# Sparse attention and a squared-ReLU layer on one core: the last four squares of the first half batch taken in place in slot 8, its last transpose on TensorE, one key load and eight output pieces moved

## The chip, the cores and the metric

The kernel runs on one core of a Trainium2 chip. The core has five engines that run side by side, each through its own list of instructions in order: TensorE (PE, matrix products; its weight loads have a row of their own, PEld), VectorE (DVE), ScalarE (ACT), GpSimd (POOL) and SyncE (SP, which here only issues transfers). They hand work to each other by semaphores. Products land in PSUM banks, which the other engines empty; everything else lies in SBUF, filled from and written to HBM by DMA.

The metric is the device time of one execution in microseconds (us). Before the change the median of three runs is 269.56 us (269.19 to 270.07).

## What is computed

Queries, keys and values have 4 batches, 8 heads, 768 tokens and 64 columns. For each query the 24 chunks of 32 keys get an upper bound of their score from each chunk's smallest and largest key; the six best chunks are kept, and attention runs over these alone, causally. The result, 3072 tokens of 512 columns, goes through a layer with a squared ReLU.

```python
ub = sum(max(q * k_min, q * k_max))        # per query and chunk, causal
top_chunks = argsort(ub)[..., -6:]
scores = where(chunk of key in top_chunks and key <= query, q @ k.T / 8, -1e9)
x = softmax(scores) @ v                     # reordered to 3072 x 512
h = maximum(x @ w_in, 0)                    # 512 -> 2048
out = (h * h) @ w_out                       # 2048 -> 512
```

## The kernel before

**Slots.** Work is cut into 32 slots, numbered from 0. A slot is one pair of heads for 384 queries, which is half of a batch. Four slots make a half batch, `hb = s // 4`; `ORDER` puts them as batch 0 first half (slots 0 to 3), batch 1 first half (4 to 7), batch 0 second half (8 to 11), batch 1 second half (12 to 15), and so on. "The ninth slot" is slot 8, and "the tenth pair" belongs to slot 9. A manual schedule is used: each engine runs its instructions in the order in which the program text issues them. The loop over slots (from 4 on) is that order, written by hand.

**Attention of a slot.** For slot `s` the loop runs, among others:

- `step_E(s, hh, n)` (L452, L458, L462): scores of head `hh`, bank `n`, on PE into a PSUM tile `ps`; ACT takes the exponent into `e`; for `n == 1` POOL zeroes the part above the diagonal (the affine select).
- `step_U(s+1)` (L375, L382, then DVE L389, L391): the bounds `ub` of the next slot on PE, the maxima and the choice of chunks on DVE.
- `step_V(s+1)` (L434, L439): the choice turned by PE into `qt`, copied by DVE into the queries' extra rows of `kq`.
- `step_F(s-1)` (L478, then DVE L487, L488): the product with the values, `po`, for the slot before, and its division into `x`.
- `step_P(s+2)` (L267): keys and queries of the slot after next turned by PE into `tk` and `tq`; then `relus_T` (ACT, L288), `extrema` (DVE, L228 to L233: smallest and largest keys) and `place` (L293: keys by DVE, queries by ACT). For slot 9 these last steps stand at the head of slot 8 instead, around `step_F(7)`.

From half batch 3 on (`ON_PE`), keys and queries are not turned by PE but by transposes of DMA that SP issues (`tr`, L320, into `kqT`). For half batch 3 the loads are `load_n` (L109, issued by POOL): three of keys (`j` = 0, 1, 2) in slot 7, three of queries in slot 8. SP issues the three transposes of keys at the start of slot 9, the three of queries at the start of slot 10, and `place_dma` (L306) at the start of slot 11. On SP's list the transpose of `x` of slot 8 stands between the keys' and the queries' transposes. The readers are DVE: `step_K` (L336, smallest and largest keys of half batch 3, from slot 10 on) and `relus` (L316, L317, `qr` of slot 12), which `step_U(12)` in slot 11 needs.

**The layer.** `x` of a half batch is turned into `xT`: pair by pair by a transpose of DMA that SP issues right after `step_F` (L492), except for half batch 0, where PE does it (`x_T`, L516, into a PSUM tile `pt` that DVE copies, `x_copy`, L522). `push(hb)` then puts the layer's pieces of that half batch in a queue: 16 "up" pieces (`ffn_up`, L563: four matmuls of 384 columns into `ph`, ReLU by ACT into `ht`, L567, the square by DVE into `h`, L569) and 12 "down" pieces (`ffn_down`, L581: four matmuls of 512 columns into `py`, three tiles `t` of four steps `c`; step `c` needs the squares 4c to 4c+3; the last step is followed by a copy to `ob`, L587, and the write to `out`, L591). The downs of a half batch are queued among the ups of the next one; the first four of them follow its own ups at once (`LAG`). `f1()` takes one piece off the queue, if the slot's `quota` allows; so these pieces fill PE between the steps of the attention.

PSUM is tight: `psF` has two banks (`ph`, in the first slots also `tk`, `pt`, and the second output tile of half batch 0), `psY` one (`py`, and for slots 5 to 8 the transposed keys or queries), `psS` three (`ps`), `psA` two (`ub`, `qt`, `po`, later `tq`). In slot 7, piece (0, 0) of the downs takes the bank of `psY` that holds `tk` of slot 8 until DVE has copied it (L293).

**Numbers that the change touches.** `quota` by pair: half batch 1 (5, 5, 4, 4), half batch 2 (8, 6, 7, 5). Through slot 7 the queue has given up pieces 0 to 15 of half batch 0 and the downs (0, 0), (0, 1); (1, 0) and (1, 1) follow in slot 8.

Of the kernel before, what the change touches and what calls it, by code (L numbers as in the profile page):

```python
# [9 lines left out]
BF16 = mybir.dt.bfloat16  # L10
AX = mybir.AxisListType
ALU = mybir.AluOpType
ACT = mybir.ActivationFunctionType
# [4 lines left out]
HB = HT * 128  # L18
# [21 lines left out]
def kernel(  # L40
# [9 lines left out]
    nc = tc.nc  # L50
# [3 lines left out]
    NP = H // 2  # L54
# [3 lines left out]
    NFI = DFF // 128  # L58
# [153 lines left out]
    def col_of(half, j, i):  # L212
        for n, bank in enumerate(BANKS[half]):
            for (at, jj, i0, m) in bank:
                if jj == j and i0 <= i < i0 + m:
                    return 512 * n + at + 128 * (i - i0)
        raise KeyError

    slots = [(b, half, p) for b, half in ORDER for p in range(NP)]
    NS = len(slots)  # L220
# [16 lines left out]
    def in_order(x):  # L237

        return x.rearrange("r (j p) -> r p j", j=TP)

    def by_token(x):
        return x.rearrange("r (p j) -> r p j", j=TP)
# [47 lines left out]
    def place(s, n, copy, h0=0, h1=2):  # L290
        b, half, p = slots[s]
        for h in range(h0, h1):
            copy(by_token(kqs[b % 2][0:D, p, 2 * half + "kq".index(n), h, :]),  # L293
                 in_order(st[s][n][D * h:D * h + D]))
# [54 lines left out]
    F, Y, A = (psF, "ph"), (psY, "py"), (psA, "att")  # L349
# [92 lines left out]
    def step_E(s, hh, n):  # L442
# [17 lines left out]
        if n == 1:  # L460
# [2 lines left out]
                out=d, in_=d, compare_op=ALU.is_ge, fill=0.0, base=0,  # L463
                channel_multiplier=-1, pattern=[[0, 3], [1, 128]])

    xs = {}

    def step_F(s, hh):
        b, half, p = slots[s]
        t = st[s]  # L470
        if hh == 0:
            t["po"] = psA.tile([128, 2, HT, D + 1], F32, tag="att", name="po")
        po = t["po"]
        for i in range(HT):
            iq = HT * half + i
            for j in range(iq + 1):
                c = col_of(half, j, iq)
                nc.tensor.matmul(  # L478
                    po[:, hh, i, :], lhsT=t["e"][hh][:, c:c + 128],
                    rhs=vn[b % 2][:, 2 * p + hh, j, :],  # L480
                    start=(j == 0), stop=(j == iq))
        if hh == 1:
            if p == 0:
                xs[s // NP] = work.tile([128, NP, HT, 128], BF16, tag="x", name="x")
            x = xs[s // NP]
            r = work.tile([128, 2, HT, 1], F32, tag="r", name="r")
            nc.vector.reciprocal(r, po[:, :, :, D:D + 1])  # L487
            nc.vector.tensor_mul(  # L488
                x[:, p].rearrange("p j (h d) -> p h j d", h=2),
                po[:, :, :, 0:D], r.to_broadcast([128, 2, HT, D]))  # L490
            if s // NP and s < NS - 1:
                nc.sync.dma_start_transpose(  # L492
                    out=xT_of(s // NP)[:, p, :].rearrange("r (j t) -> r j t", j=HT),
                    in_=x[:, p].rearrange("p j t -> p (j t)"))
            st.pop(s)
# [3 lines left out]
    h2 = {}  # L499
# [3 lines left out]
    def xT_of(hb):  # L503
        if hb not in xTs:
            xTs[hb] = late.tile([128, NKI, HB], BF16, tag="xT", name="xT")
        return xTs[hb]
# [3 lines left out]
    def x_T(hb, g, pt, us=(0, 1)):  # L510

        if (hb, g) not in pts:
            pts[hb, g] = pt[0].tile([128, 2, HB], BF16, tag=pt[1], name="pt")
        for u in us:
            for j in range(HT):
                nc.tensor.matmul(  # L516
                    pts[hb, g][:, u, 128 * j:128 * (j + 1)],
                    lhsT=xs[hb][:, 2 * g + u, j, :],
                    rhs=ident, is_transpose=True, start=True, stop=True)

    def x_copy(hb, g, u0, u1, copy):
        copy(xT_of(hb)[:, 2 * g + u0:2 * g + u1, :], pts[hb, g][:, u0:u1, :])  # L522

    def push(hb):
        xT = xTs.pop(hb)
        xs.pop(hb)
        ups = [lambda act, f=f: ffn_up(hb, xT, f) for f in range(NFI)]
        for c in ("u" * NFI if hb == 0 else
                  "dddd" + "uuud" * 4 + "uuuu" if hb < 2 * B - 1 else
                  "uudddd" + "uuud" * 4 + "uu"):  # L530
            queue.append((ups if c == "u" else downs).pop(0))
        downs.extend(ffn_downs(hb, int(hb == 2 * B - 1)))
        if hb < 2 * B - 1:
            queue.extend(downs.pop(0) for _ in range(LAG))

    def ffn_downs(hb, tail=False):
        py = {}
        order = [(t, c) for t in range(HT - tail) for c in range(4)]
        if hb == 0:

            order = [(0, 0), (0, 1), (1, 0), (1, 1), (0, 2), (0, 3), (1, 2), (1, 3)] + order[8:]
        return [lambda act, t=t, c=c: ffn_down(hb, py, t, c, act, tail) for t, c in order]

    def ffn_last(hb):
# [15 lines left out]
    def ffn_up(hb, xT, f):  # L560
        ph = psF.tile([128, 512], F32, tag="ph", name="ph")
        for ki in range(NKI):
            nc.tensor.matmul(  # L563
                ph[:, 0:HB], lhsT=w_in[:, ki, 128 * f:128 * (f + 1)],
                rhs=xT[:, ki, :], start=(ki == 0), stop=(ki == NKI - 1))
        ht = late.tile([128, HB], BF16, tag="ht", bufs=4, name="ht")
        nc.scalar.activation(ht, ph[:, 0:HB], ACT.Relu)  # L567
        h = late.tile([128, HB], BF16, tag="h", bufs=2 * NFI + 2, name="h")
        nc.vector.tensor_mul(h, ht, ht)  # L569
        h2[hb, f] = h  # L570

# [29 lines left out]
    def at(s, fn, *a):  # L601
        later.setdefault(s, []).append(lambda: fn(*a))
# [21 lines left out]
        at(3 + g, load_w_out, 8 * g, 8 * g + 8)  # L624
    for j in range(HT):
        at(6, load_vt, 0, HT + j)
        at(7, load_n, "k", 3, j)
        at(8, load_n, "q", 3, j)
        at(9, load_vt, 1, HT + j)
    at(9, codes, 1, 1, nc.gpsimd.dma_start)  # L630
# [59 lines left out]
    late = ctx.enter_context(tc.tile_pool(name="late", bufs=2))  # L690
# [44 lines left out]
    for s, (b, half, p) in enumerate(slots):  # L735
        if s < NP:
            continue
        hb = s // NP
        nb = len(BANKS[half])
        hf = nb // 2  # L740
        quota = [((5, 5, 4, 4) if hb == 1 else (8, 6, 7, 5) if hb == 2 else (8, 6, 7, 7))[p]]
        for fn, *a in first.get(s, ()):
            fn(*a)
        if (hb == ON_PE - 1 and p == 2) or (ON_PE < hb < 2 * B - 1 and p == 0):
# [2 lines left out]
        def f1():  # L747
            if quota[0] and queue:
                quota[0] -= 1
                fill(1, True)  # L750
# [12 lines left out]
        if s == 2 * NP:  # L763
            for n in range(hf):
                step_E(s, 0, n)
            relus_T(s + 1)
            place(s + 1, "q", nc.scalar.copy)
            step_F(s - 1, 0)
            step_F(s - 1, 1)
            push(1)  # L770
            f1()
            f1()
            extrema(s + 1)
            place(s + 1, "k", nc.vector.tensor_copy)
        if p == 0 and hb > 2:
            step_F(s - 1, 0)
            step_F(s - 1, 1)
            push(hb - 1)
        else:
            f1()  # L780
# [26 lines left out]
                .rearrange("p i h j c -> p (i h j) c"), 0.0)  # L807
        late_f = half == 0 and hb > 2
        border = p == 0 and hb > 1
        if not border and not (late_f and p == NP - 1):  # L810
            f1()
        if p and s > NP:
            step_F(s - 1, 0)
# [88 lines left out]
```

## Time and profile before

The profiled execution took 269.26 us; its span, from the first to the last instruction, is 267.5 us. The median of the runs shown is 0.30 us above that execution.

| | busy us | share of the span | instructions |
|---|---|---|---|
| PE (matmul) | 254.6 | 95% | 2406 |
| PEld (weight load) | 156.3 | 58% | 2406 |
| DVE | 163.4 | 61% | 617 |
| ACT | 177.5 | 66% | 398 |
| POOL | 93.6 | 35% | 140 |

How it is read: a row of the timeline gives start, length, engine, line, operation, names and shapes, and how many instructions were merged; in square brackets stand the idle time of the engine just before and what is taken to have ended it. Matmuls overlap, so a row's length reaches into the next row. The granted clock of PE was full in all of the 40 slices. A row "in windows" gives, for a stretch of time, the busy time of each engine in it.

### The profile page before, as it was taken

How to read it: one execution, taken by the hardware profiler on the slowest of the kernel's cores; microseconds unless marked ns; L12 is line 12 of the kernel's file. 1: busy time of each engine (PE TensorE's matmuls, PEld its weight loads, DVE VectorE, ACT ScalarE, POOL GpSimd, SP SyncE). 2: the span in 40 equal slices, each digit the busy share in tenths (PEclk: the TensorE clock that was granted, in tenths of full speed). 3: DMA queues.
4: the chain of work that ended last, by engine and by line, in shares of the span. 5: the costliest groups of instructions: out<-in, count | busy, mean ns of one | idle time of the engine just before them, and what ended most of it. 6: DMA issues, size and time to landing. Idle time of an engine off the chain costs nothing.

```text
span 267.5 us, 6575 instructions
## 1 busy us (share of the span) xinstructions
PE 254.6 (95%) x2406; PEld 156.3 (58%) x2406; DVE 163.4 (61%) x617; ACT 177.5 (66%) x398; POOL 93.6 (35%) x140
## 2 busy tenths in 40 slices
PE   7878998889999999999999999999999999999995
PEld 6565554446656566665565566655565566645543
DVE  6789998565997458656875567455863233424411
ACT  4888986597895578845575787944685788614500
POOL 8897455524931325325521444220120111000000
PEclk9999999999999999999999999999999999999999
DMA  7999999999997599999996899998542220111022
GB/s 141 159 175 182 207 214 193 113 165 117 133 131 158 124 151 185 121 195 141 187 153 137 130 145 176 109 164 144 134 101 69 71 44 18 54 43 39 0 81 78
DMA packets 116849, 33.98 MB, mean 127 GB/s; under 512 B 103760, under 2 KB 112752, under 8 KB 116816
## 3 DMA queue, kind: packets, MB, share of 16 engines
q0 software_dynamic: 64672, 13.83, 72.4%
q1 hardware_dynamic: 51200, 19.33, 41.0%
q10 hardware_dynamic: 944, 0.39, 0.6%
q8 instruction: 19, 0.31, 0.5%
q14 instruction: 14, 0.11, 0.2%
HBM read 27.26 MB, written 6.29 MB: 125 GB/s over the span
## 4 chain that ended last, share of the span: by engine, by line
PE 75%; DVE 7%; DMA 6%; issue 4%; ACT 4%; POOL 3%; POOLq 0%; DVEq 0%; ACTq 0%
PE py L581 26%; PE ph L563 24%; PE ps L452 10%; PE po L478 7%; DMA xT<-x 3%; DMA kn<-in_k_dram 3%; PE idle L657 2%; ACT e L458 2%; POOL kn L109 1%; PE ub L375 1%; PE py L551 1%; ACT ht L567 1%; POOL e L462 1%; DVE km L336 1%; DVE x L488 1%
## 5 line engine op out<-in xcount | busy, mean ns | idle before, releaser
L458 ACT ACTIVATE e<-ps 128x512 bf16<-128x512 f32 x192 | 96.4, 552 | 19.3 <-PE ps L452 18.4
L563 PE MATMUL ph<-xT,w_in 128*128 128x384 bf16 x512 | 98.7, 325 | 1.7 <-DMA xT<-x 1.2
L581 PE MATMUL py<-w_out,h 128*128 128x512 bf16 x368 | 88.1, 379 | 0.9 <-DVE kq L293 0.7
L567 ACT ACTIVATE ht<-ph 128x384 bf16<-128x384 f32 x128 | 62.4, 500 | 28.6 <-PE ph L563 27.8
L569 DVE TENSOR_TENSOR h<-ht 128x384 bf16<-128x384 bf16 x128 | 46.6, 375 | 55.8 <-ACT ht L567 55.2
L462 POOL TENSOR_SCALAR_AFFINE_SELECT e<-e 128x384 bf16<-128x384 bf16 x64 | 34.1, 538 | 125.8 <-ACT e L458 122.2
L563 PEld LDWEIGHTS <-w_in 128*128 128x128 bf16 x512 | 47.7, 97 | 32.7 <-issue 2.7
L452 PE MATMUL ps<-kq 96*128 96x384 bf16 (+2 forms) x320 | 57.4, 278 | 2.1 <-DVE kq L428 2.1
L581 PEld LDWEIGHTS <-h 128*128 128x128 bf16 x368 | 34.6, 97 | 35.9 <-DVE kq L293 0.8
L452 PEld LDWEIGHTS <-kq 96*128 96x128 bf16 x320 | 26.3, 97 | 16.9 <-issue 2.2
L478 PEld LDWEIGHTS <-e 128*128 128x128 bf16 x672 | 25.4, 98 | 6.2 <-POOL e L462 1.6
L478 PE MATMUL po<-vn,e 128*128 128x65 bf16 x672 | 27.0, 194 | 1.6 <-POOL e L462 1.0
L587 ACT COPY ob<-py 128x512 f32<-128x512 f32 x18 | 10.5, 585 | 25.4 <-PE py L581 25.1
L389 DVE MAX8 m<-ub 128x8 f32<-128x16 f32 (+4 forms) x160 | 16.1, 166 | 17.0 <-PE ub L382 11.1
L488 DVE TENSOR_TENSOR x<-po,r 128x384 bf16<-128x384 f32 x32 | 17.8, 557 | 1.1
L109 POOL DMA_DIRECT2D kn<-in_k_dram x15 | 13.4, 901 | 3.0 <-ACT e L458 2.6
L109 POOL DMA_DIRECT2D qn<-in_q_dram x15 | 13.2, 889 | 0.3
L125 POOL DMA_DIRECT2D vn<-in_v_dram x15 | 12.5, 840 | 2.2 <-ACT qr L288 2.0
L336 DVE TENSOR_TENSOR km<-km 128x384 bf16<-128x384 bf16 (+3 forms) x40 | 12.2, 304 | 1.1
L375 PE MATMUL ub<-kbd,qr 128*128 128x48 bf16 (+1 forms) x160 | 9.9, 180 | 1.5 <-DVE kbd L233 0.9
L375 PEld LDWEIGHTS <-qr 128*128 128x128 bf16 x160 | 7.8, 96 | 5.6 <-DVE qr L316 1.5
L288 ACT ACTIVATE qr<-tq 128x256 bf16<-128x256 bf16 (+1 forms) x24 | 8.8, 422 | 0.9 <-PE tq L260 0.7
(71 smaller groups left out, 178.0 us busy)
## 6 DMA issues: line engine op xcount, KB each, us to landing
out_dram<-ob SPq DMA_DIRECT2D x23, 256.0 KB, 2.5
w_in<-in_moe_w_in_dram POOLq DMA_DIRECT2D x2, 1024.0 KB, 12.2
w_out<-in_moe_w_out_dram POOLq DMA_DIRECT2D x2, 1024.0 KB, 19.3
kn<-in_k_dram POOLq DMA_DIRECT2D x15, 128.0 KB, 6.7
qn<-in_q_dram POOLq DMA_DIRECT2D x15, 128.0 KB, 6.7
kq<-kqT SPq DMA_DIRECT2D x10, 192.0 KB, 5.3
vn<-in_v_dram POOLq DMA_DIRECT2D x4, 384.0 KB, 8.4
vn<-in_v_dram POOLq DMA_DIRECT2D x9, 128.0 KB, 9.7
```

What stands on the lines that cost most here:

```text
L109: nc.gpsimd.dma_start(out=nat_of(n, g)[:, DM * j:DM * j + DM].rearrange("p (h d) -> p h d", d=D), in_=rows(n, *ORDER[g], 0, H)[:, 128 * j: ...
L375: nc.tensor.matmul(ub[:, j - j0], lhsT=st[s]["qr"][:, w, 128 * j:128 * (j + 1)], rhs=kbds[b % 2][:, p, w, :, 0:ncs], start=bool(half) and ...
L389: nc.vector.max(out=m8[:, j, hh, :], in_=ub[:, j - j0, hh, 0:12 * half + 4 * j + 4])
L452: nc.tensor.matmul(ps[:, at:at + 128 * m], lhsT=kqs[b % 2][0:KR, p, 2 * (j // HT), hh, 128 * (j % HT):128 * (j % HT + 1)], rhs=qc(s, hh)[: ...
L458: nc.scalar.activation(e[:, 512 * n + lo:512 * n + hi], ps[:, lo:hi], ACT.Exp, scale=float(scale))
L462: nc.gpsimd.affine_select(out=d, in_=d, compare_op=ALU.is_ge, fill=0.0, base=0, channel_multiplier=-1, pattern=[[0, 3], [1, 128]])
L478: nc.tensor.matmul(po[:, hh, i, :], lhsT=t["e"][hh][:, c:c + 128], rhs=vn[b % 2][:, 2 * p + hh, j, :], start=(j == 0), stop=(j == iq))
L488: nc.vector.tensor_mul(x[:, p].rearrange("p j (h d) -> p h j d", h=2), po[:, :, :, 0:D], r.to_broadcast([128, 2, HT, D]))
L563: nc.tensor.matmul(ph[:, 0:HB], lhsT=w_in[:, ki, 128 * f:128 * (f + 1)], rhs=xT[:, ki, :], start=(ki == 0), stop=(ki == NKI - 1))
L567: nc.scalar.activation(ht, ph[:, 0:HB], ACT.Relu)
L569: nc.vector.tensor_mul(h, ht, ht)
L581: nc.tensor.matmul(py[t], lhsT=h2[hb, f][:, 128 * t:128 * (t + 1)], rhs=w_out[:, f, :], start=(f == 0), stop=(f == NFI - 1))
```

## The change

- **Squares.** The last four up pieces of half batch 0 (`f` = 12 to 15) no longer square at once. ACT writes the ReLU straight into `h`, the square is kept in a list `squares`, and DVE takes the four in place in slot 8, behind `extrema` and `place` of slot 9's keys. Before, two of them stood in slot 6 and two in slot 7 on DVE.
- **Last transpose of half batch 1.** For slot 7, SP no longer transposes `x`; PE does it (`x_T`, three matmuls into a bank of `psF`), and DVE copies it into `xT` behind the four squares. `push(1)` stands behind that copy.
- **Order of pieces.** In slot 7 no piece is taken ahead of `step_F(6)`. The downs of half batch 0 run (0,2), (1,2), (0,3), (1,3) instead of (0,2), (0,3), (1,2), (1,3). The queue of half batch 1 begins with six downs instead of four, then five ups, a down, five ups, a down and six ups. The quota of half batch 2 is (8, 5, 6, 7) instead of (8, 6, 7, 5).
- **One key load.** The third load of keys for half batch 3 moves from slot 7 to slot 8, and there, on POOL's list, it follows the select of `step_E(8, 1, 1)`, between the second and the third load of queries. POOL's order there becomes: two key loads, three selects, two query loads, a select, the key load, the third query load.

Everything that is computed stays; SP issues one transpose less, PE three matmuls more, DVE one copy more.

```diff
@@ step_F
-            if s // NP and s < NS - 1:
+            if s // NP and s < NS - 1 and s != 2 * NP - 1:
                 nc.sync.dma_start_transpose(
@@ push
         for c in ("u" * NFI if hb == 0 else
+                  "dddddd" + "u" * 5 + "d" + "u" * 5 + "d" + "u" * 6 if hb == 1 else
                   "dddd" + "uuud" * 4 + "uuuu" if hb < 2 * B - 1 else
@@ ffn_downs
-            order = [(0, 0), (0, 1), (1, 0), (1, 1), (0, 2), (0, 3), (1, 2), (1, 3)] + order[8:]
+            order = [(0, 0), (0, 1), (1, 0), (1, 1), (0, 2), (1, 2), (0, 3), (1, 3)] + order[8:]
@@ ffn_up
+        h = late.tile([128, HB], BF16, tag="h", bufs=2 * NFI + 2, name="h")
+        if hb == 0 and f >= NFI - 4:
+            h2[hb, f] = h
+            nc.scalar.activation(h, ph[:, 0:HB], ACT.Relu)
+            squares.append(lambda: nc.vector.tensor_mul(h, h, h))
+            return
         ht = late.tile([128, HB], BF16, tag="ht", bufs=4, name="ht")
         nc.scalar.activation(ht, ph[:, 0:HB], ACT.Relu)
-        h = late.tile([128, HB], BF16, tag="h", bufs=2 * NFI + 2, name="h")
         nc.vector.tensor_mul(h, ht, ht)
@@ loads
-        at(7, load_n, "k", 3, j)
+        at(7 + j // 2, load_n, "k", 3, j)
@@ loop over slots
-        quota = [((5, 5, 4, 4) if hb == 1 else (8, 6, 7, 5) if hb == 2 else (8, 6, 7, 7))[p]]
+        quota = [((5, 5, 4, 4) if hb == 1 else (8, 5, 6, 7) if hb == 2 else (8, 6, 7, 7))[p]]
@@ s == 2 * NP
             step_F(s - 1, 0)
             step_F(s - 1, 1)
-            push(1)
-            f1()
+            f1()
+            x_T(1, 1, F, (1,))
             f1()
             extrema(s + 1)
             place(s + 1, "k", nc.vector.tensor_copy)
+            for fn in squares:
+                fn()
+            x_copy(1, 1, 1, 2, nc.vector.tensor_copy)
+            push(1)
@@ ahead of step_F
-        if not border and not (late_f and p == NP - 1):
+        if not border and not (late_f and p == NP - 1) and s + 1 != 2 * NP:
             f1()
```

1 line of the change is left out of this document (added).

## The prediction, made before the changed kernel had run

> **What bounds the kernel now.** I read the shares of the engines first, then the windows, to see where PE stands still, then PE's timeline there. PE is the busiest engine, and after 85.14 us it is idle for 174.86 - 174.47 = 0.39 us in all: nothing is to be had there. Between 42.00 and 60.49 us it is idle for 18.49 - 15.11 = 3.38 us, in the next stretch for 0.47.
>
> ```profile
> PE 254.6 (95%) x2406; PEld 156.3 (58%) x2406; DVE 163.4 (61%) x617; ACT 177.5 (66%) x398; POOL 93.6 (35%) x140
> 42.00:60.49 18.49, 15.11 (x142) 8.26 (x140) 12.41 (x42) 12.39 (x28) 8.26 (x12) 1.00 2.62 154
> 60.49:85.14 24.65, 24.18 (x287) 15.93 (x285) 20.55 (x84) 19.74 (x44) 12.21 (x17) 1.00 1.62 139
> 85.14:260.00 174.86, 174.47 (x1484) 103.75 (x1482) 93.58 (x359) 110.44 (x239) 42.98 (x62) 1.00 0.92 112
> ```
>
> PE's timeline names four waits in the first stretch, and they are all of it: 0.47 + 0.72 + 0.99 + 1.20 = 3.38. In order: the bounds of slot 8 wait for DVE, the first down piece for DVE's copy of keys (which frees its bank), the second head of `step_F(7)` for POOL's select, an up piece of half batch 1 for the transpose of `x`.
>
> ```profile
> 43.10 0.31 PE L375 MATMUL ub<-kbd,qr 128*128 128x48 bf16 x6 [0.47 <-DVE kbd L233]
> ...
> 44.14 1.04 PE L581 MATMUL py<-w_out,h 128*128 128x512 bf16 x4 [0.72 <-DVE kq L293]
> 45.01 0.54 PE L478 MATMUL po<-vn,e 128*128 128x65 bf16 x12
> 45.39 1.03 PE L581 MATMUL py<-w_out,h 128*128 128x512 bf16 x4
> ...
> 49.34 0.36 PE L478 MATMUL po<-vn,e 128*128 128x65 bf16 x6 [0.99 <-POOL e L462]
> 49.54 3.61 PE L581 MATMUL py<-w_out,h 128*128 128x512 bf16 x16
> 52.99 0.55 PE L452 MATMUL ps<-kq 96*128 96x128 bf16 x3
> ...
> 58.94 1.71 PE L563 MATMUL ph<-xT,w_in 128*128 128x384 bf16 x9 [1.20 <-DMA xT<-x]
> ```
>
> So a change here is worth what it takes off these four, less what it makes PE wait elsewhere.
>
> **Squares out of slots 6 and 7.** On DVE two of them stand ahead of slot 8's keys:
>
> ```profile
> 39.75 0.35 DVE L569 TENSOR_TENSOR h<-ht 128x384 bf16<-128x384 bf16 x1
> ...
> 40.71 0.35 DVE L569 TENSOR_TENSOR h<-ht 128x384 bf16<-128x384 bf16 x1
> ...
> 42.97 1.11 DVE L293 COPY kq<-tk 64x384 bf16<-64x384 bf16 x2
> 44.00 0.61 DVE L569 TENSOR_TENSOR h<-ht 128x384 bf16<-128x384 bf16 x2
> ```
>
> DVE has no idle time there, so without a pair (0.61 merged) everything behind it is 0.61 earlier: the bounds no longer wait 0.47, and the copy of keys ends at 44.08 - 0.61 = 43.47. PE is free for the down piece 0.47 earlier too, at 44.14 - 0.72 - 0.47 = 42.95, and the change puts `step_F(6)` there (45.39 - 45.01 = 0.38), which fills the wait: down piece at 43.5, end at 43.5 + 0.87 = 44.4, where before piece and product ended at 45.39. Gain 1.0.
>
> **The third key load out of slot 7.** It holds POOL until 48.74, when the select starts for which PE waits 0.99:
>
> ```profile
> 47.85 0.89 POOL L109 DMA_DIRECT2D kn<-in_k_dram  x1 [2.62 <-ACT e L458]
> 48.74 1.04 POOL L462 TENSOR_SCALAR_AFFINE_SELECT e<-e 128x384 bf16<-128x384 bf16 x2
> ...
> 55.79 0.52 POOL L462 TENSOR_SCALAR_AFFINE_SELECT e<-e 128x384 bf16<-128x384 bf16 x1 [4.17 <-ACT e L458]
> 56.26 0.88 POOL L109 DMA_DIRECT2D qn<-in_q_dram  x1
> ```
>
> The load itself had waited 2.62; the exponent named is not its input, so I take that wait as one for an older transfer. The select now follows its exponent alone. What remains of the wait lies between 0 and 0.99; I take 0.1, since PE gets one head of `po` done (0.19) while ACT and POOL finish. Gain 0.9, so `po` of slot 7 ends 1.9 earlier. The query loads that now come first on POOL gate nothing in this slot.
>
> **Transpose of slot 7's `x` on PE.** Rows from the end of the kernel, where the same three matmuls run once:
>
> ```profile
> 234.16 0.33 PE L516 MATMUL pt<-ident,x 128*128 128x128 bf16 x3
> 234.33 1.89 PE L581 MATMUL py<-w_out,h 128*128 128x512 bf16 x8
> ...
> 49.97 0.56 DVE L488 TENSOR_TENSOR x<-po,r 128x384 bf16<-128x384 f32 x1
> ```
>
> The matmuls cost 234.33 - 234.16 = 0.17. They need `x`, whose end (50.53) was 1.19 after the second head of `po` began (49.34); PE fills 0.20 + 0.87 of that with `po` and one down piece: a wait of 0.13. Cost 0.3. In return the chain
>
> ```profile
> 50.56 8.34 DMA xT<-x
> ```
>
> is gone, and with it 1.20: slot 7's part of `xT` is ready when DVE has copied it, and PE now has all eight downs to do ahead of the first up piece. Slots 4 to 6 keep their transposes; slot 6's starts about 1 us earlier, at 45.4, and even a flight as long as this one would land before 57.
>
> **Squares into slot 8.** DVE must do 4 squares (row below) and the copy of `xT` behind slot 9's keys, ahead of the maxima of slot 9:
>
> ```profile
> 79.42 1.16 DVE L569 TENSOR_TENSOR h<-ht 128x384 bf16<-128x384 bf16 x4
> ...
> 53.74 0.61 DVE L389 MAX8 m<-ub 128x8 f32<-128x16 f32 x6 [1.03 <-PE ub L382]
> ```
>
> DVE was idle for 1.03 there; 1.16 + 0.35 (a square's 0.35 stands for the copy) is 0.5 more than this cover, and the choice of chunks still has about 0.5 until PE's `qt` (down piece (1,3) now stands ahead of it). Down piece (0,3) needs all four: I put their end at 51.8 and PE's arrival at 52. Cost 0, margin 0.2. No row shows an in-place square; bounds 0.29 each, as here, and twice that.
>
> Sum at the start of slot 9: 1.0 + 0.9 - 0.3 + 1.2 = 2.8 earlier.
>
> **Order of pieces in slots 9 to 11.** An up piece costs 0.65, a down 0.87 (rows below). By the new quota and order PE comes to the bounds of slot 12 with two up pieces (1.3) fewer behind it, and does these later in slot 11. But that spot is set by DVE:
>
> ```profile
> 61.09 0.86 PE py L581 x4
> 61.96 0.65 PE ph L563 x4
> ...
> 66.57 0.37 PE L267 MATMUL tk<-ident,kn 96*64 96x96 bf16 x8
> ...
> 67.81 0.56 DVE L228 TENSOR_REDUCE km<-tk 128x12 bf16<-128x384 bf16 x1
> ...
> 78.58 0.26 DVE L316 TENSOR_SCALAR qr<-kqT 128x384 bf16<-128x384 bf16 x1 [0.21 <-DMA kqT<-qn]
> 78.76 0.58 DVE L317 TENSOR_SCALAR qr<-kqT 128x384 bf16<-128x384 bf16 x1
> ...
> 79.39 0.30 PE L375 MATMUL ub<-kbd,qr 128*128 128x48 bf16 x5 [0.30 <-DVE qr L317]
> ```
>
> From slot 11's keys (67.81) to the end of the second ReLU (79.34) DVE works 11.5 us nearly without a gap, and it starts when PE has turned the keys (66.57). That point moves by the 2.8 and by 0.2 for an up in a down's place; so the bounds run at 79.39 - 3.0 = 76.4 and PE waits over 1 us for them. With 1.3 of pieces still to do there, 1.7 of the gain is left; these pieces then fill what PE idled up to slot 12 (of the 0.47 at most; DVE is 3.0 ahead, so no wait there is due). Between 0 and 0.5 comes back from it, and as much again if rows' tails hide more idle time than the brackets name: I take 0.5. Left: 2.2.
>
> The sum against the profiled execution: 269.26 - 2.2 = 267.06; that execution is 0.30 under the median of the runs. I forecast 267.1. The bounds: no gain above (3.38 + 0.47 - 0.3) = 3.5, so 265.8; and if the bounds of slot 12 give back 1 us more, 268.3.
>
> **Rivals.** *The third key load is late (the slower side).* It is now issued behind the select of slot 8's last head: 55.79 less some 1.5 puts it at 54.8 instead of 47.85. On SP, in order, its transpose (1.2 long) stands ahead of slot 8's `x` and of the queries' transposes, and these set the ReLU at 78.58:
>
> ```profile
> kn<-in_k_dram POOLq DMA_DIRECT2D x1, 128.0 KB, 10.3
> qn<-in_q_dram POOLq DMA_DIRECT2D x1, 128.0 KB, 7.3
> vn<-in_v_dram POOLq DMA_DIRECT2D x1, 128.0 KB, 4.0
> ...
> 65.88 1.18 SPq L492 DMA_TRANSPOSE xT<-x  x1
> 67.16 5.07 SPq L320 DMA_TRANSPOSE kqT<-qn  x3
> ```
>
> The first row (last number: us to landing) is that load before, the second the query load issued at 56.26, the third a value load issued at 62.76. To keep 3 us, SP must be free for slot 8's `x` at 62.9, so the load must land by 61.7, 6.9 after its issue. With 7.3 it costs 0.4, within my range. At 10.3 it lands at 65.1, the queries' transposes start about 67.6, later than before, and by the same us-for-us count the 2.2 become 2.2 - 3.4 = -1.2: 270.5. It decides from 6.9 + 2.2 = 9.1 on (no gain left). For it: the transposes of the other two key loads and two output writes are under way then; against it: the ring that held it up has one load less ahead of it.
>
> The Trainium skill, "DMA: Bandwidth & Descriptors", section "Queues, rings and completion order", says that each DMA engine serves its rings in turn, a packet at a time. By that rule the load shares the engines with SP's transfers for its whole flight, and the sum would be that of 10.3, 270.5; by the row of 7.3, whose load also flew beside key transposes, it is 267.5. The trace bears the rule out in direction: the value load, with less beside it, took 4.0.
>
> *In-place squares at twice the price.* Then they end at 53, piece (0,3) and the choice of slot 9 each come 1 us late, one behind the other's cover: 268.1. Against it: the operands are those of the rows, only the target differs.
>
> *DVE gives nothing back.* If PE's wait at the bounds of slot 12 is filled, the 2.8 and the 0.47 stay: 266.0. Against it: DVE's run of 11.5 us.
>
> *The change moves the wait only.* With a flight of 8.3 to 9.9 that load leaves between 0.8 gained and 0.8 lost: no change, 269.3.
>
> **How the numbers follow.** Forecast 0.57, squares at twice the price 0.10, nothing given back 0.05: together 0.72 faster by over 0.3% (0.8 us, about what can be told from no change). The load late: 0.13 no change, 0.15 slower. The range leaves out the best case's edge (0.04) and most of the slow one (0.14): 265.9 to 269.5. The forecast's own range is 266.0 to 268.3.
>
> **What would show it.** Right: PE's brackets at the bounds of slot 8, at `po` of slot 7 and at the first `ph` of half batch 1 are gone or under 0.2; `ps` behind the first downs of slot 8 begins near 51.3; the first scores of slot 9 come 2.8 earlier, at equal pieces; PE waits about 1 us for `qr` before the bounds of slot 12, with no DMA named. Wrong: a wait of DVE for `kqT` over 0.5 us, or PE waiting for `h` at a `py` in slot 8, or SP's transpose of slot 8's `x` later than 63.5.

## The result, and the profile after

The changed kernel took 268.53 us (median of 22 runs, 267.75 to 270.07); the kernel before, 22 runs beside them, 270.88. The ratio is 0.9946, 95% interval 0.9923 to 0.9968: faster by 0.5%, which on 269.56 us is 1.5 us, where 2.46 were forecast. Profiled execution against profiled execution it is less still: 268.67 (span 266.9) after 269.26 (span 267.5), so 0.6 against the 2.2 of the sum. The ratios leave out executions in the chip's slower state, nearly all of them of the kernel before (it spread from 268 to 276 us in these and the later runs, the changed one from 268 to 271), so they are not the quotients of the medians; versions are compared below by their spans and by medians taken on one chip.

Where the time went is seen best if the stretch that the change touches is cut at fixed steps of PE: the `tq` transposes that end slots 6, 7, 8 and 9, and the first scores of slot 12, `step_E(12, 0, 0)`. First the windows of the kernel before (length, PE busy with its number of matmuls, then PEld, DVE, ACT, POOL, granted clock, DMA share, GB/s):

```profile
40.53:47.26 6.73, 5.54 (x69) 3.21 (x63) 5.93 (x21) 4.27 (x12) 3.66 (x5) 1.00 1.50 189
47.26:56.78 9.52, 8.53 (x84) 4.59 (x79) 5.12 (x19) 6.30 (x15) 4.67 (x7) 1.00 3.49 116
56.78:66.76 9.98, 8.78 (x106) 5.50 (x101) 6.14 (x22) 8.17 (x19) 3.03 (x5) 1.00 1.60 147
66.76:84.55 17.79, 17.32 (x211) 11.39 (x207) 16.60 (x66) 14.74 (x33) 9.54 (x14) 1.00 1.74 151
```

and those of the changed kernel:

```profile
40.57:46.29 5.72, 5.40 (x69) 3.19 (x63) 4.67 (x17) 4.43 (x12) 2.98 (x5) 1.00 1.39 173
46.29:55.09 8.80, 8.78 (x87) 4.68 (x82) 6.49 (x24) 6.30 (x14) 3.48 (x6) 1.00 2.75 140
55.09:63.83 8.74, 8.74 (x106) 5.51 (x101) 5.81 (x21) 7.47 (x18) 4.19 (x6) 1.00 1.32 145
63.83:83.86 20.03, 17.25 (x211) 11.26 (x206) 16.87 (x68) 15.07 (x34) 9.44 (x14) 1.00 1.87 147
```

PE does the same work in the four stretches together (40.17 us in each). Its idle time (length less busy) was 1.19, 0.99, 1.20 and 0.47; it is now 0.32, 0.02, 0.00 and 2.78. So the first three stretches give 26.23 - 23.26 = 2.97 us, and the fourth takes 2.24 of them back. After the first scores of slot 12 the two kernels are alike (182.95 and 183.04 to the end).

PE's timeline of the changed kernel shows both halves:

```profile
42.51 0.31 PE L375 MATMUL ub<-kbd,qr 128*128 128x48 bf16 x6
...
43.54 1.04 PE L589 MATMUL py<-w_out,h 128*128 128x512 bf16 x4 [0.32 <-DVE kq L293]
...
47.03 0.62 PE L480 MATMUL po<-vn,e 128*128 128x65 bf16 x12
...
48.53 0.34 PE L518 MATMUL pt<-ident,x 128*128 128x128 bf16 x3
48.71 2.75 PE L589 MATMUL py<-w_out,h 128*128 128x512 bf16 x12
51.30 0.55 PE L452 MATMUL ps<-kq 96*128 96x128 bf16 x3
...
57.12 0.81 PE L566 MATMUL ph<-xT,w_in 128*128 128x384 bf16 x4
...
76.24 0.47 PE L375 MATMUL ub<-kbd,qr 128*128 128x48 bf16 x6 [1.17 <-DVE qr L316]
...
83.86 0.60 PE L452 MATMUL ps<-kq 96*128 96x384 bf16 x4 [1.60 <-DMA kq<-nsel]
```

Down to 76.24 this is what the prediction drew: the waits at the bounds of slot 8, at `po` and at the first `ph` are gone, the down piece starts at 43.54 (forecast 43.5), the scores behind the first downs of slot 8 at 51.30 (51.3), the bounds of slot 12 at 76.24 (76.4), with a wait of 1.17 (over 1). The last row is new. The first scores of slot 12 wait 1.60 us for `kq`, written by a DMA from `nsel`. This is `step_W(12)` (L413): SP's transpose that puts the queries and the choice of slot 12 into `kq`. SP's timeline after:

```profile
72.60 1.37 SPq L306 DMA_DIRECT2D kq<-kqT  x2
74.02 0.63 SPq L599 DMA_DIRECT2D out_dram<-ob  x1
78.33 1.43 SPq L413 DMA_TRANSPOSE kq<-nsel  x1
```

and before:

```profile
75.59 1.38 SPq L306 DMA_DIRECT2D kq<-kqT  x2
77.55 0.34 SPq L591 DMA_DIRECT2D out_dram<-ob  x1
81.59 1.24 SPq L413 DMA_TRANSPOSE kq<-nsel  x1
```

The issues of DMA give its time to landing, before:

```profile
kq<-nsel SPq DMA_TRANSPOSE x1, 2.8
```

and after:

```profile
kq<-nsel SPq DMA_TRANSPOSE x1, 5.4
```

Issued 3.26 earlier, it lands only 0.7 earlier (83.7 for 84.4). Before, it landed 0.15 ahead of the scores at 84.55; after the change, the scores that wait for it begin about as long behind its landing. So there was no bracket to see, and no slack either.

### The profile page after: what moved, and what is told of

Same layout as the page of the kernel before. It is cut to its first block, busy times and chain, and to the rows that moved or that the text cites. A ratio compares the mean times of both kernels' runs of the same rounds, so it can differ in the third digit from the quotient of the medians.

```text
span 266.9 us, 6575 instructions
## 1 busy us (share of the span) xinstructions
PE 254.6 (95%) x2409; PEld 156.3 (59%) x2409; DVE 163.4 (61%) x618; ACT 177.3 (66%) x398; POOL 93.4 (35%) x140
## 4 chain that ended last, share of the span: by engine, by line
PE 79%; DVE 10%; DMA 5%; ACT 2%; issue 2%; SPq 1%; POOL 0%; DVEq 0%; POOLq 0%; ACTq 0%
PE py L589 29%; PE ph L566 24%; PE ps L452 11%; PE po L480 7%; DMA kqT<-qn 3%; DMA kq<-nsel 2%; PE idle L665 2%; PE ub L375 1%; PE py L554 1%; DVE h L577 1%; DVE kq L293 1%; PE tk L267 1%; SPq L320 1%; DVE km L336 1%; DVE x L490 1%
## 5 line engine op out<-in xcount | busy, mean ns | idle before, releaser
L577 DVE TENSOR_TENSOR h<-ht 128x384 bf16<-128x384 bf16 x124 | 45.5, 378 | 56.2 <-ACT ht L576 55.7
L576 ACT ACTIVATE ht<-ph 128x384 bf16<-128x384 f32 x124 | 60.3, 501 | 28.6 <-PE ph L566 28.1
L336 DVE TENSOR_TENSOR km<-km 128x384 bf16<-128x384 bf16 (+3 forms) x40 | 12.2, 306 | 1.1
```

## The experiments

All of them compute the whole layer. The table has, for each: chip set (1 to 5, the kernels of one set ran on one chip), median, ratio to before with its interval, span, the stretch from the `tq` that ends slot 6 to the first scores of slot 12, flight of the transpose of `nsel`, and PE's waits at the bounds of slot 12 and at its first scores (0 where no bracket names one). The kernel before had medians of 271.21, 271.85, 271.82, 270.52 and 271.86 beside the five sets. Spans, stretches, flights and waits are those of one execution each, medians those of 4 to 22.

| run | set | median us | ratio [95%] | span | stretch | flight | waits |
|---|---|---|---|---|---|---|---|
| before | | 270.88 | | 267.5 | 44.02 | 2.8 | 0.30, 0 |
| after | | 268.53 | 0.9946 [0.9923, 0.9968] | 266.9 | 43.29 | 5.4 | 1.17, 1.60 |
| again | 1 | 268.39 | 0.9977 [0.9939, 1.0015] | 266.9 | 42.92 | 5.2 | 0.53, 1.39 |
| t_xt9 | 1 | 268.15 | 0.9985 [0.9946, 1.0024] | 266.4 | 42.89 | 5.0 | 1.19, 1.19 |
| t_place | 1 | 270.07 | 1.0007 [0.9961, 1.0054] | 269.3 | 45.78 | 2.7 | 2.39, 0 |
| t_q4 | 1 | 266.71 | 0.9894 [0.9832, 0.9956] | 264.6 | 40.79 | 2.8 | 0.54, 0 |
| b_q4 | 2 | 268.52 | 0.9849 [0.9785, 0.9913] | 266.8 | 42.81 | 2.8 | 0.31, 0 |
| u_sq | 2 | 268.78 | 0.9859 [0.9796, 0.9923] | 267.1 | 43.14 | 5.2 | 0.55, 1.45 |
| q4_u_sq | 2 | 267.30 | 0.9806 [0.9742, 0.9870] | 265.0 | 41.52 | 2.8 | 0.57, 0 |
| u_xt | 2 | 269.40 | 0.9885 [0.9793, 0.9978] | 268.1 | 42.69 | 5.7 | 0.57, 1.90 |
| u_kn | 3 | 270.34 | 0.9980 [0.9930, 1.0031] | 266.9 | 43.21 | 5.2 | 1.22, 1.41 |
| q4_u_kn | 3 | 268.27 | 0.9933 [0.9899, 0.9966] | 266.5 | 42.44 | 2.8 | 0.92, 0 |
| u_quota | 3 | 268.36 | 0.9926 [0.9882, 0.9969] | 267.8 | 42.78 | 4.5 | 0.30, 1.64 |
| q4_quota | 3 | 266.90 | 0.9889 [0.9843, 0.9935] | 264.8 | 41.14 | 3.0 | 0.20, 0 |
| q4_again | 4 | 266.49 | 0.9890 [0.9855, 0.9925] | 264.7 | 40.99 | 2.8 | 0.57, 0 |
| b_q4_again | 4 | 268.50 | 0.9957 [0.9921, 0.9993] | 267.9 | 44.47 | 2.8 | 1.49, 0 |
| q4_u_xt | 4 | 266.20 | 0.9875 [0.9829, 0.9920] | 264.6 | 40.62 | 2.8 | 0.57, 0 |
| t_pl10 | 5 | 269.41 | 0.9973 [0.9922, 1.0024] | 267.3 | 43.77 | 5.9 | 0.74, 2.14 |
| t_out | 5 | 266.76 | 0.9824 [0.9774, 0.9875] | 265.5 | 41.17 | 3.5 | 0.53, 0 |
| t_both | 5 | 267.97 | 0.9874 [0.9808, 0.9940] | 268.1 | 43.97 | 2.8 | 1.96, 0 |

Four of the profiled executions lost time to the granted clock, whatever their edit. Between the bounds and the first scores of slot 12 it was 0.77 in t_place (79.11 to 86.57) and in t_both (77.69 to 85.12). PE was busy there for 7.46 and 7.43 us, in t_out for 5.84 with the same work: 1.6 of these two stretches is no effect of the edits. In u_xt (0.69 from 24 to 28 us, behind a wait of 0.82 for `w_in`) and in u_quota (0.75 from 83.12 to 90) the drop lies outside the stretch; there the span alone is longer, by 1.5 and 1.6.

### First set: what does the transpose of nsel wait for?

Two theories stood at the start. By A it stands behind other transfers on SP's own queue; by B POOL's six loads for half batch 4 take the DMA engines from it.

**again**: the changed kernel unaltered.

> The changed kernel once more, as the yardstick of this set. Both theories: about 0.5% under before (ratio 0.993 to 0.997), PE waiting 1.2 us for the ReLU of slot 12's queries at L375 and 1.6 us at the first scores of slot 12 for the transpose of its queries (kq from nsel).

The wait is there again, 1.39 with a flight of 5.2; the one at the bounds is 0.53, not 1.2, and the ratio lies just above what was expected.

**t_xt9**: SP's transpose of slot 9's `x` is held back until the transpose of `nsel` has been issued.

```diff
+            if s == 2 * NP + 1:
+                held.append(turn)
...
             step_W(s + 1)
+            for fn in held:
+                fn()
```

> SP's transpose of slot 9's x is issued behind the transpose of slot 12's queries instead of 7 us ahead of it. Theory A (SP's own transfers ahead of it on the same ring hold the transpose of slot 12's queries back): it lands 1 to 2.5 us earlier after its issue (flight 3 to 4.4 instead of 5.4 us), PE's wait of 1.6 at slot 12 falls to under 0.6, time 1 to 1.6 us under the changed kernel. Theory B (the flight is long because POOL's loads for half batch 4 share the DMA engines): flight and time as in the changed kernel within 0.4 us.

The flight is 5.0 and the wait 1.19: almost nothing. That transposition is not what it waits behind.

**t_place**: POOL copies the keys of half batch 3 into `kq`, so that two of SP's transfers (384 KB) fall away.

```diff
-            nc.sync.dma_start(
+            (nc.gpsimd.tensor_copy if g == ON_PE else nc.sync.dma_start)(
```

> The two copies of half batch 3's keys into kq (192 KB each, 7 to 8 us in flight) are taken by POOL instead of SP's DMA. Theory A: the transpose of slot 12's queries lands 2 us earlier, the wait of 1.6 at slot 12 is gone, time 1.3 to 1.6 us under the changed kernel. Theory B: change under 0.5 us. If POOL's copies take over 4 us, its select for slot 11 comes late and PE waits there instead, which would show at step_F(11).

The flight falls to 2.7, but `nsel` itself comes 2.9 us later (81.21), so the run doesn't show which transfers had mattered for it (what it shows of the write is used in the fifth set). The cost sits elsewhere: DVE's rows in this kernel,

```profile
74.77 1.29 DVE L336 TENSOR_TENSOR km<-kqT 128x768 bf16<-128x768 bf16 x1
76.10 2.47 DVE L336 TENSOR_TENSOR km<-km 128x384 bf16<-128x384 bf16 x4
```

beside POOL's

```profile
74.15 3.25 POOL L306 COPY kq<-kqT 64x1536 bf16<-64x1536 bf16 x2
```

took 0.56 and 1.46 in the changed kernel:

```profile
73.12 0.56 DVE L336 TENSOR_TENSOR km<-kqT 128x768 bf16<-128x768 bf16 x1
73.71 1.46 DVE L336 TENSOR_TENSOR km<-km 128x384 bf16<-128x384 bf16 x4
```

So on the way to the bounds of slot 12 DVE took 1.7 us longer while POOL's copies ran; that they are the cause is read from the overlap alone. Another operation of L336, ahead of the copies, took 1.58 for 0.65, and what held it is not shown.

**t_q4**: POOL issues the three loads of queries for half batch 4 a slot later, so that they start at 79.80 and not at 69.37 (the two empty entries keep the order of what else is issued there).

```diff
+    for _ in range(2):
+        at(11, len, ())
...
-            at(4 * g - (7 if g == 4 else 8) + i // HT, load_n, "kq"[i // HT], g, i % HT)
+            at(4 * g - (7 if g == 4 else 8) + i // HT + (g == 4 and i >= HT), load_n, "kq"[i // HT], g, i % HT)
```

> The three query loads of half batch 4 (128 KB each, issued at 69 to 72 us and landing by 82) are issued one slot later, behind the select of slot 11's last head, at about 80. Theory A: flight of slot 12's transpose stays over 4.8 us, time within 0.4 us of the changed kernel. Theory B: the flight falls to under 4 us and the time by 1 us or more.

PE's timeline of this kernel has no wait at slot 12:

```profile
75.70 0.46 PE L375 MATMUL ub<-kbd,qr 128*128 128x48 bf16 x6 [0.54 <-DVE qr L316]
...
80.59 1.12 PE L480 MATMUL po<-vn,e 128*128 128x65 bf16 x30
81.55 0.60 PE L452 MATMUL ps<-kq 96*128 96x384 bf16 x4
```

and the transpose takes 2.8 again, as theory B had it. 268.39 became 266.71 on one chip, 1.7 us, by moving three loads that have nothing to do with slot 12.

### Second set: the same loads in the kernel before, and two steps undone

**b_q4**: the same edit on the kernel before.

> The kernel before, with only half batch 4's query loads issued one slot later. Theory B1 (these loads cost nothing before, since the transpose of slot 12's queries landed just when PE came to slot 12, and cost only once PE came earlier): within 0.5 us of before. Theory B2 (the loads already held the kernel before back): 1 us or more under before.

No wait for these loads goes from the profiled execution: its span is 0.7 under before, but slot 8 alone is 1.0 shorter in it (8.50; the select's wait is missing, and why is seen in the third set). The repetition in the fourth set has a span of 267.9. The runs speak for B2 rather. The ratio is 0.9849 for these four and 0.9957 [0.9921, 0.9993] for the twelve of the repetition, so by the larger sample the late loads are worth some 1.2 us to the kernel before as well. Its shortest executions hardly gain (267.88 of the twelve, 268.13 of the 22 before beside them); what becomes rare is its long ones, and no profile here shows what those waited for.

**u_sq** (on the changed kernel) and **q4_u_sq** (on the version with late query loads): the four squares are taken at once again.

```diff
-        if hb == 0 and f >= NFI - 4:
+        if False:
```

> The changed kernel with the four squares taken at once again, on DVE in slots 6 and 7. Theory P (what a step gains arrives at the end): the bounds of slot 8 wait again, PE is 0.5 to 1.0 us later at slot 8 and the time 0.5 to 1.0 above the changed kernel. Theory D (the start of slot 12 is set by DMA): PE is as late at slot 8, but its wait at slot 12 shrinks by most of that, and the time rises by less than 0.4.

> Squares at once, with half batch 4's query loads one slot later. Both theories: no wait at slot 12 to hide in, so 0.5 to 1.0 us above the run with the late loads and the squares in place (span 264.6), that is a span of 265.1 to 265.6.

In both, slot 7 is 6.25 long instead of 5.72, so the squares are worth 0.53 there. At the end this is 0.2 of span in the first and 0.3 to 0.4 in the second, where 0.5 to 1.0 was expected.

**u_xt**: SP turns the `x` of slot 7 again.

```diff
-            if s // NP and s < NS - 1 and s != 2 * NP - 1:
+            if s // NP and s < NS - 1:
...
-            x_T(1, 1, F, (1,))
...
-            x_copy(1, 1, 1, 2, nc.vector.tensor_copy)
```

> The changed kernel with slot 7's x turned by SP's DMA again instead of PE. The order of the pieces puts the first up piece 1.7 us of downs later than before, and x is about 1.6 us earlier at about 48.5 us. By the flight of 8.3 us it lands at 57 and PE comes to it at 56.9: a wait of 0 to 0.5 us there. Theory P: time within -0.2 to +0.5 us of the changed kernel. Theory D: within 0.3 either way, since slot 12 is set elsewhere.

The execution came to slot 7 1.5 us late, for the wait and the clock told above, so its span can't be used; but its first `ph` had no wait for `xT`.

### Third set: the key load and the quota undone

**u_kn** and **q4_u_kn**: the third key load back in slot 7.

```diff
-        at(7 + j // 2, load_n, "k", 3, j)
+        at(7, load_n, "k", 3, j)
```

> The changed kernel with the third key load of half batch 3 back in slot 7, ahead of the select of its last head. All theories: the wait of PE for that select in slot 7 comes back (0.7 to 1.0). Theory P (each step's gain reaches the end of the kernel): span 0.9 over that of the changed kernel, 267.8. Theory D (the start of slot 12 is held by the transpose of nsel, which shares the DMA engines with POOL's loads for half batch 4): PE's waits at the bounds of slot 12 and at its scores, 1.9 to 2.1 together in the changed kernel, take up part of it; span at most 0.5 over, 267.0 to 267.4, with a wait for kq of nsel at the first scores of slot 12 and a flight of that transpose of 5 us.

> The same undo on the version whose last three query loads for half batch 4 come a slot later. Theory D: no wait at the scores of slot 12 takes it up, so the undo costs nearly its whole 0.9: span 265.3 to 265.6 against 264.6 of that version, flight of the transpose of nsel 2.8. Theory P: 0.9 as well, so that this run tells the theories apart only beside the undo on the changed kernel: by P the two undos cost the same, by D this one costs more by 0.4 at least.

The two executions differ in something that neither theory had named. POOL's timeline of the first:

```profile
45.40 0.89 POOL L109 DMA_DIRECT2D kn<-in_k_dram  x1 [0.32 <-DMA w_out<-in_moe_w_out_dram]
```

and of the second:

```profile
47.32 0.89 POOL L109 DMA_DIRECT2D kn<-in_k_dram  x1 [1.91 <-DMA w_out<-in_moe_w_out_dram]
```

The load waits for a load of `w_out` on POOL's list, for 0.32 or 1.91 us. In the first case the select isn't held up, and slots 7 and 8 are as long as in the changed kernel. In the second PE waits 1.01 at `po`; slot 8 is 9.91 long instead of 8.80, and the span 1.9 more, twice what was expected. What the step is worth depends on when `w_out` lands: between 0 and over 1 us in these two executions. That u_kn's profile shows no loss does not mean that its runs had none: their median, 270.34, is 2.0 over that of u_quota on the same chip. Longer waits for `w_out` in them would explain it, but no profile shows that.

**u_quota** and **q4_quota**: the quota of half batch 2 as before.

```diff
-(8, 5, 6, 7) if hb == 2
+(8, 6, 7, 5) if hb == 2
```

> The changed kernel with the quota of half batch 2 as before, (8, 6, 7, 5): two up pieces more ahead of the bounds of slot 12, two fewer behind them. The prediction's step: the wait at the bounds goes, the gain of 2.8 stays: 0.5 to 1 faster. Theory D: PE comes to the bounds 1.3 later and finds no wait there, the choice and so the transpose of nsel start 0.5 to 0.8 later, and PE has two pieces fewer while it flies: the wait at the scores of slot 12 grows to 2 to 2.7, span the same to 0.8 over (266.9 to 267.7).

> The same quota on the version with the late query loads. Theory D: the transpose of nsel flies 2.8 us, and with the bounds some 0.75 later lands near 81.3, about when PE comes (81.0): the 0.54 at the bounds goes and at most 0.3 comes back at the scores, span 264.3 to 264.6. If the bounds' place were what sets the end in both versions (theory P), it is 0.5 faster here and in the changed kernel alike.

In the changed kernel the wait moves from the bounds (1.17 or 0.53, now 0.30) to the scores (1.64), and the stretch stays (42.78 against 42.92 and 43.29); the span is longer by the clock alone. With late query loads it is 0.15 to 0.35 longer, and the span 264.8 for 264.6 and 264.7. So the wait of over 1 us that the prediction took for the price of the order of pieces is not what sets the end.

### Fourth set: the change alone, side by side

**q4_again**, **b_q4_again** and **q4_u_xt** (the late query loads on the changed kernel, on the kernel before, and on the changed kernel with SP's transpose of slot 7's `x`).

> The changed kernel with the three query loads of half batch 4 one slot later, again, so that it stands beside the next two on one chip. Theory D (what held the start of slot 12 were these loads): 266.7, span 264.6, and 1.5 to 2.2 under the next one, which is what the prediction's sum forecast for the change (2.2). If the change itself were worth only what was measured of it, 1.4 on the medians, the difference would be that or less.

> The kernel before with the same late loads. Theory D: nothing waits for these loads there, so it stays within 0.5 of before in its profiled execution and 1.5 to 2.2 above the version before it in this list.

> The version with the late loads, and the x of slot 7 turned by SP's transpose again, so without the matmuls of pt and the copy behind the squares. By the prediction the transpose of DMA costs a wait at the first ph of at most 1.2 and saves 0.3 of PE: 0.9 slower. But all eight downs now stand ahead of that ph, and the undo on the changed kernel showed no wait there: then it is 0.3 faster to the same, span 264.3 to 264.7.

With these loads out of the way in both, the change gives 268.50 - 266.49 = 2.0 us on one chip. The spans of the single executions say 3.2, but that one of b_q4_again had a wait of its own: 1.49 at the bounds of slot 12, where DVE waited 1.81 for the turned queries. The shortest runs tell the same: with the late loads the change gives 267.88 - 266.21 = 1.7, without them (the 22 runs each of the result) 268.10 - 267.75 = 0.35. The medians without them hide it (270.88 - 268.53 = 2.35), because they hold the long executions of the kernel before, which the late loads also make rare.

The third run goes against the prediction, as its expectation had allowed: without PE's transpose it isn't slower but has the lowest median of all, 266.20. Its first `ph`,

```profile
57.16 0.81 PE L566 MATMUL ph<-xT,w_in 128*128 128x384 bf16 x4
```

does not wait. All eight down pieces now stand ahead of it, and the transpose of DMA lands in their time; the matmuls of `pt` and their wait only cost (slot 8 is 8.44 without them, 8.80 with).

### Fifth set: how do POOL's loads hold up SP's transpose?

POOL's loads could slow the transpose itself, or SP's earlier transfers, behind which it stands. The packets of the changed kernel between issue and landing, 78.33 to 83.7 (packets, MB, their time as a share of 16 engines' span; q0 is POOL's queue, q1 SP's), speak for the second:

```profile
q1 hardware_dynamic: 2001, 0.89, 116.2%
q0 software_dynamic: 81, 0.01, 2.9%
```

POOL's loads were nearly done, and SP's queue had 0.89 MB to move. In the 4.3 us ahead of the issue, 74 to 78.33, it had been the other way round:

```profile
q0 software_dynamic: 3072, 0.39, 225.4%
q1 hardware_dynamic: 584, 0.22, 44.9%
```

while with late query loads, in the 4.3 us ahead of the issue there (73.5 to 77.8), SP's queue had moved three times as much:

```profile
q1 hardware_dynamic: 739, 0.67, 87.3%
q0 software_dynamic: 71, 0.01, 3.2%
```

**t_pl10** issues the two placements of keys (384 KB) a slot earlier; **t_out** issues the write of output at 74.02 (256 KB) behind the transpose of `nsel`; **t_both** does both. POOL's loads stay.

```diff
-    first.setdefault(s0 + 2, []).append((place_dma, ON_PE))
+    first.setdefault(s0 + 1, []).append((place_dma, ON_PE))
```

```diff
-            nc.sync.dma_start(out[r0:r0 + 128, :], ob)
+            def write(r0=r0, ob=ob):
+                nc.sync.dma_start(out[r0:r0 + 128, :], ob)
+            if (hb, t) == (0, 2):
+                held.append(write)
+            else:
+                write()
...
             step_W(s + 1)
+            for fn in held:
+                fn()
```

> The changed kernel with the two placements of half batch 3's keys (384 KB, SP) at the start of slot 10, behind the three transposes of queries, rather than of slot 11; POOL's loads stay where they are. Theory E (what the transpose of nsel waits for is the backlog on SP's own queue: 0.89 MB of SP's packets ran during its 5.4 us, and only 81 packets of POOL's): the backlog is 384 KB less, the flight 2.8 to 4, the wait at slot 12 at most 0.6, span 265.4 to 266.2. Theory F (POOL's loads slow that transpose itself): flight 5 and wait 1.4 to 1.6 as they were, span 266.4 to 266.9.

> The changed kernel with the one write of output of slot 11 (256 KB, SP) issued behind the transpose of nsel instead of 4 us ahead of it. Theory E: 256 KB less ahead of it, of the 0.89 MB: flight 3.5 to 4.3, wait 0.3 to 0.9, span 265.6 to 266.3. Theory F: no difference, 266.4 to 266.9.

> Both of these on the changed kernel. Theory E: 640 KB less ahead of the transpose of nsel, flight near the 2.8 of the version with the late query loads, wait 0 to 0.3, span 264.8 to 265.4. Theory F: 266.4 to 266.9.

With the write alone out of the way the wait is gone. PE's timeline of t_out:

```profile
81.50 1.12 PE L481 MATMUL po<-vn,e 128*128 128x65 bf16 x30
82.46 0.60 PE L452 MATMUL ps<-kq 96*128 96x384 bf16 x4
```

its issues between 74 and 84 us:

```profile
out_dram<-ob SPq DMA_DIRECT2D x1, 256.0 KB, 4.3
...
kq<-nsel SPq DMA_TRANSPOSE x1, 3.5
```

and its packets in the 4.1 us ahead of that issue, 74.6 to 78.71, with POOL still the larger share:

```profile
q0 software_dynamic: 3175, 0.40, 165.4%
q1 hardware_dynamic: 607, 0.24, 43.8%
```

So A and B each held one half. POOL's loads don't slow the transpose directly (in its flight they moved 0.01 MB): they slow what stands ahead of it on SP's queue, the placements and the write of output. In the changed kernel that write took 7.8 us, and landed at 74.02 + 7.8 = 81.8; with the loads late 4.3. But the loads alone don't do it either. In t_place the two placements are gone, and the write took

```profile
out_dram<-ob SPq DMA_DIRECT2D x1, 256.0 KB, 4.4
```

while POOL's queue moved 0.46 MB in those 4.4 us (73.72 to 78.12), more than in the 4.3 us shown for the changed kernel. The write is slow where both come together, loads beside it and placements ahead of it. t_pl10 fell short of both expectations: the placements, issued 3.3 us earlier, took 8.5 instead of 7.8, the write came out no faster (8.2), and the flight was 5.9. Issuing bytes earlier didn't help here; taking them off the queue ahead of the transpose did. In t_both the flight is 2.8, but the placements now delay the turned queries, for which DVE waits 1.29, and PE 1.96 at the bounds; its profiled execution is the longest of its four (269.85, the others 266.75 to 268.31).

The Trainium skill, "DMA: Bandwidth & Descriptors", section "Queues, rings and completion order", has both halves of this: an engine takes turns between the rings that have work, and within one ring goes by order, the completion signal only after that engine's earlier writes. The trace agrees: SP's queue got through 0.22 MB beside POOL's loads and 0.67 MB without them, and the transpose landed 1.9 us behind the write ahead of it.

## Why the prediction was wrong, by its own steps

The direction was right and 268.53 lies within 265.9 to 269.5; the size was 1 us off on the runs and 1.6 on the profiled execution.

- *Squares out of slots 6 and 7, gain 1.0.* Slot 7 went from 6.73 to 5.72: 1.01. 0.53 of it are the squares (u_sq); the other 0.48 is left for `step_F(6)` ahead of the down piece, by subtraction, since no run undoes that alone. The bank's wait was to vanish; 0.32 of it stayed.
- *Third key load, gain 0.9.* The select's wait is gone (slot 8: 0.99 idle, now 0.02). But the load's own 0.89 isn't what held PE up (in u_kn it cost nothing); it is the wait ahead of it, which the prediction took for one on an older transfer and which the runs name: `w_out`, 0.32 to 2.23. So the gain is no constant: nothing in the execution of u_kn, over 1 us in that of q4_u_kn; the same kernel waited 0.50 in b_q4 and 2.23 in b_q4_again.
- *Transpose on PE, cost 0.3, and 1.20 in return.* The 1.20 is gone, and slot 8's balance of 0.99 - 0.3 = 0.7 was 0.72. The credit was given to the wrong edit: the eight downs ahead of the first `ph` do it alone (q4_u_xt, u_xt), and PE's transpose is a net cost of about 0.3 (266.49 with it, 266.20 without; 0.36 in slot 8).
- *Squares in slot 8, cost 0.* Right. DVE's rows after:

```profile
50.58 1.15 DVE L573 TENSOR_TENSOR h<-h 128x384 bf16<-128x384 bf16 x4
51.76 0.36 DVE L524 COPY xT<-pt 128x384 bf16<-128x384 bf16 x1
52.05 0.61 DVE L389 MAX8 m<-ub 128x8 f32<-128x16 f32 x6
```

  1.15 in place where 1.16 stood for four with another target: the rival of twice the price falls.
- *Sum at the start of slot 9, 2.8, and 0.2 more in slot 9.* The first scores of slot 9 came 2.72 earlier (57.77 for 60.49), and it is 2.97 by the end of slot 9.
- *Bounds of slot 12 at 76.4, PE waiting over 1 us.* 76.24 and 1.17; in the repetition 0.53, since DVE's own wait of 0.44 for `kqT` is missing there.
- *"these pieces then fill what PE idled up to slot 12 (of the 0.47 at most; DVE is 3.0 ahead, so no wait there is due)".* **This is the step that failed.** DVE was ahead, but the scores of slot 12 also need a transfer, and this one came only 0.7 earlier: a wait of 1.60, where none was due. Without it they would stand at 83.86 - 1.60 = 82.26, 2.29 earlier than before; the sum said 2.2. Two different edits that take this wait away, the late query loads (266.71 and 266.49) and the late write (266.76), bring the changed kernel below the 267.1 that was forecast. With late query loads in both kernels the difference is 2.0 on one chip. The rest of the sum held in its total, with the credits shifted as said. None of the three signs named for being wrong came (DVE's wait for `kqT` was 0.44): they all lay ahead of the bounds of slot 12, the loss behind them.
- *The rivals.* The late key load didn't come: it was issued at 54.83, as forecast, and flew 5.5 us, not 10.3; SP's transpose of slot 8's `x` stood at 62.96, where 62.9 was asked for. What the prediction took from the trace for sharing between rings was weak: beside the value load that flew 4.0, SP's queue moved 0.19 MB in those 4.0 us, beside the key load that flew 10.3 only 0.22 MB in all; it was POOL's own queue that was busier there. What did come was its mechanism at another place: transfers of POOL's and SP's queues on the same engines, and one on SP's list late for PE. The prediction followed SP's list up to the queries' transposes and stopped one transfer short of the one with no slack.

While the wait at slot 12 stands, undoing one part of the change moves the stretch by no more than 0.6 (u_sq 43.14, u_xt 42.69, u_kn 43.21, u_quota 42.78, against 42.92 and 43.29); with it gone, undoing the squares costs 0.5 to 0.7 (41.52 against 40.99 and 40.79) and the key load up to 1.65 (42.44).

Open is why the write was slow after the change and less so before. The third query load is issued 6.72 us ahead of the transpose of `nsel` in both kernels (74.87 to 81.59, 71.61 to 78.33), and the write 4.0 and 4.3 us ahead; yet the write took 6.2 and 7.8. Also open is whether t_out and the late loads add up: no run combines them.

## What to carry to other kernels

Before work is moved forward, list everything that the step after it needs, transfers too, and compute for each how long ahead of its reader it lands: one without a bracket may have no slack at all (here 0.15 us), and then the gain ends there. A small transfer that PE waits for should be issued ahead of a large write on the same queue, and loads that are needed late should not be started where other queues have urgent work. An undo of one part says little while a later wait swallows every difference; take that wait away first, then undo.

## What was not expected of the hardware

A transpose of DMA of the same shape takes 2.8 or 5.4 us from issue to landing, by what stands ahead of it on its queue; the write of 256 KB ahead of it 3.6 (q4_quota) to 8.2 (t_pl10), slowest where loads of another queue and 384 KB on its own come together. Beside copies by POOL (3.25 us) DVE's two-input operations took 1.29 instead of 0.56 and 2.47 instead of 1.46. The Trainium skill, "SBUF — State Buffer", section "SBUF: two separate sides", tells of a pair of ports that DVE and GpSimd share, where one of the two is blocked; the direction agrees, while no run here shows a lock. One load on POOL's list waited between 0.32 and 2.23 us for a transfer of weights, from execution to execution, and with it a microsecond of PE's time came and went. In three executions the granted clock fell to 0.75 to 0.77 for about 7 us right behind a wait of PE of 1.64 (u_quota), 1.96 (t_both) and 2.39 (t_place), which cost 1.6 us each, and in u_xt to 0.69 behind one of 0.82; behind waits of 1.60 (the changed kernel) and 2.14 (t_pl10) it stayed full, so no rule follows from these runs.
